# Preparation work handed out between the products of a pair, and loads spread over the steps of a block, in a two-layer kernel behind chunked attention

## The chip, the core and the metric

The kernel runs on one core of a Trainium2 chip. The metric is the device time of one execution in microseconds (us), as the median of several runs. The engines are named as in the profile: PE multiplies matrices, PEld is PE's weight load, DVE is the vector engine, ACT the scalar engine, POOL GpSimd. SP issues nearly all DMAs.

## The reference

Attention within chunks of 64 tokens over (8, 8, 576, 64), then two feed-forward layers on 4608 tokens, with a model width of 512 and an inner width of 2048. All arrays are float32 or float64.

```python
scores = scale * np.matmul(q_c, k_c.transpose(0, 1, 2, 4, 3))
attn = np.exp(scores - np.max(scores, axis=-1, keepdims=True))
attn = attn / (np.sum(attn, axis=-1, keepdims=True) + 1e-09)
x = np.matmul(attn, v_c)              # to 4608 x 512
h = x @ w1_in;  x = (h * np.cos(h)) @ w1_out
h = x @ w2_in;  y = (h / (1 + np.exp(-1.702 * h))) @ w2_out
```

## The kernel before, in words

**Tiles.** The 4608 tokens are nine blocks j of 512. The inner width is sixteen slices f of 128. A float32 factor is split into a high and a low part (`split`, lines 187 to 189: ACT copies the high part, DVE subtracts to get the low one), and each product is three matmuls, high x high, high x low, low x high, of 128 rows and 512 columns. `gemm1` (line 489) makes the 128 inner values of one slice, the activation follows on ACT and DVE, and `gemm2` (line 587) adds the slice's share of the output in four accumulators. Weights come as 64-bit numbers and are converted with a chain of seven closures (`split_w_parts`, lines 206 to 259: p0 on ACT at line 214, p1 to p4 on DVE, p5 on ACT, p6 on DVE).

**Order of the stages.** In layer 0 block 0 is laid out by a planner (`Plan`), blocks 1 and 2 are plain steps (gemm1 of a slice, activation, extra work, gemm2 of the slice two before). Blocks 3 and 4, 5 and 6, 7 and 8 are done jointly, in three rounds q = 0, 1, 2 (`by_1024`, line 880): eight pairs of slices (`pair_of_slices`, line 808), in which the two slices of two blocks need seven products in place of eight, and then sixteen steps with gemm2 alone for the second block of the two. Layer 1 has one plain block and four joint ones.

**A pair.** The products are made in the order 1, 0, 2, 3, 5, 4, 6, six matmuls each, in the PSUM tiles `pb`, `pu` and `pc` (line 820). Between them stands the fill: 24 matmuls of gemm2 of the pair before (`run(6)` after product 2, `run(10)` after 5, `run(8)` after 4). Products 0, 3, 4 and 6 all add to the same tile `pu`. So the sum c11 must be taken out of it before product 3 adds to it, the copy c12 before product 4, the sum c22 before product 6. The sums are DVE additions (`plus`, line 835, tile `part`), the copies ACT's (`copied`, line 831). Four activations follow (`act_second`, lines 787 to 793). The left factors of a pair (combinations of weights) are loaded from DRAM a pair ahead (`load_factors`, line 733); the right ones (combinations of x, `right_factor`, line 739) stay in SBUF for a round: b11, b21 and b22 are x itself, split, and t1 to t4 are differences (line 758), each formed and then split.

**Preparation.** The left factors of layer 1 are prepared during layer 0's pairs, in 24 slots (three rounds of eight pairs). Each of eight pairs of weight slices takes four stages in four slots, from slots 0, 2, 4, 8, 10, 12, 16, 18 (`PREP`, `prepare1`, line 715): load both slices, convert one, convert the other, form the factors and store them (`left_factors`, line 652, DVE at 664, store at 676). So slots 3, 5, 11, 13 and 19 hold the factors of one pair of slices and the conversion of another; slots 7, 15 and 21 hold factors alone. All of a slot's work stands behind its pair in the program. The factors of x for the first joint round come in step 13 (b22) and step 15 (the others) of block 2.

**What orders the queues.** PE's order is that of the program (`manual_schedule` for PE, by hand in the program). The compiler orders the other engines and SP. The scratch tiles `t`, `r`, `wt`, `su`, `sw`, `part`, `chain`, `yo` share eight buffers (pool `tmp`, tag t).

**The last round's steps.** In round q = 2, x of layer 1 is loaded and split, and weights of layer 1 are loaded: the input weights from the stored factors (`load_w1`, line 709, 14 of 16 slices in these steps), the first nine slices of the output weights raw (`load_w`, line 196), four of them converted. Layer 0's own output weights come three steps ahead (`load_wo`, line 700, into four tiles).

Of the kernel before, what the change touches and what calls it, by code (L numbers as in the profile page):

```python
# [9 lines left out]
F32 = mybir.dt.float32  # L10
# [9 lines left out]
P = 128  # L20
# [92 lines left out]
def tile_chunk_attention_two_moe(  # L113
# [29 lines left out]


    SJ1 = ((0, 3, 5), (7, 10, 12))
    SJ2 = ((0, 3, 4), (1, 5, 6), (7, 10, 11), (8, 12, 13))
    SJ3 = ((0, 3, 4), (1, 5, 6), (4, 7, 8), (5, 9, 10))
    SR = (8, 10)

# [37 lines left out]
    def split(hi, lo, src):  # L187
        nc.scalar.activation(out=hi, in_=src, func=AF.Copy)  # L188
        nc.vector.tensor_tensor(out=lo, in0=src, in1=hi.bitcast(F32), op=ALU.subtract)  # L189
# [433 lines left out]
    def at(key, fn, *args):  # L623
        extra.setdefault(key, []).append((fn, args))
# [27 lines left out]
    def left_factors(layer, i, t, parts):  # L652

        H2 = DM // 2
        u = tp.tile([P, DM], F32, tag="t", name="su")
        w = tp.tile([P, DM], F32, tag="t", name="sw")
        add, sub = ALU.add, ALU.subtract
        for o, x, y, op in (
            (u[:, :H2], t[1][:, :H2], t[1][:, H2:], add),
            (u[:, H2:], u[:, :H2], t[0][:, :H2], sub),  # L660
            (w[:, :H2], t[0][:, :H2], t[1][:, :H2], sub),
            (w[:, H2:], t[0][:, H2:], u[:, H2:], sub),
        ):
            nc.vector.tensor_tensor(out=o, in0=x, in1=y, op=op)
        todo = [(A11, parts[0]), (A21, parts[1])]
        for k, src in ((0, u), (1, w)):
            if layer == 0:
                hi, lo = (tp.tile([P, DM], F32R, tag="t", name="s_part") for _ in range(2))
            else:
                both = wp.tile([P, 2 * DM], F32R, tag=f"i{NF - 2 + k}", name="s_part")  # L670
                hi, lo = both[:, :DM], both[:, DM:]
            split(hi, lo, src)
            todo.append((A_S1 + 2 * k, (hi, lo)))
        for at_op, both in todo:
            for part in range(2):
                nc.sync.dma_start(
                    out=wc[layer][i][part, :, at_op:at_op + 2, :]
                    .rearrange("p o c -> p (o c)").bitcast(F32),
                    in_=both[part].bitcast(F32),
                )  # L680

    def left_factors0(i):
        parts = [W[0, "i", 2 * i + k] for k in range(2)]
        t = []
        for hi, lo in parts:
            x = tp.tile([P, DM], F32, tag="t", name="w32")
            nc.vector.tensor_tensor(out=x, in0=hi.bitcast(F32), in1=lo.bitcast(F32), op=ALU.add)
            t.append(x)
        left_factors(0, i, t, parts)

    def store_wo(f):
        hi, lo = W[0, "o", f]
# [22 lines left out]
    def prepare1(i, stage):  # L715

        fs = (2 * i, 2 * i + 1)
        for k, f in enumerate(fs):
            if stage == 0:
                load_w(w2_in, 1, "i", f, tag=f"o{k}")  # L720
            elif stage == 1 + k:
                for fn in split_w_parts(1, "i", f, False, tag=f"o{2 + k}"):
                    fn()
        if stage == 3:
            left_factors(1, i, [T.pop(f) for f in fs], [W[1, "i", f] for f in fs])

    LF = {}

# [32 lines left out]
    RIGHT = [(m, k) for m in (0, 1, 2, 3, 6, 5, 4) for k in range(2)]  # L761

    RIGHT_A = [(5, k) for k in range(2)]
    RIGHT_B = [(m, k) for k in range(2) for m in (1, 0, 2, 3, 6, 4)]

    PARK = {}

# [37 lines left out]
        if f < NF:  # L805
            split(*new_g((layer, j, f)), PARK.pop(f))

    def pair_of_slices(layer, ja, i, fill):

        jb = ja + 1  # L810
        f1, f2 = 2 * i, 2 * i + 1
        lf = LF.pop(i)

        def product(m, a, out, start, stop):
            for k in range(2):
                w = slice(k * P, (k + 1) * P)
                ah, al = lf[0][:, a, w], lf[1][:, a, w]
                bh, bl = RF[m][0][:, k], RF[m][1][:, k]
                for n, (x, y) in enumerate(((ah, bh), (ah, bl), (al, bh))):
                    nc.tensor.matmul(  # L820
                        out=out, lhsT=x, rhs=y,
                        start=(start and k == 0 and n == 0), stop=(stop and k == 1 and n == 2), skip_group_check=True,
                    )

        def run(count):
            for _ in range(min(count, len(fill))):
                fill.pop(0)()

        def copied(src):
            t = tp.tile([P, N], F32, tag="t", name="part")  # L830
            nc.scalar.activation(out=t, in_=src, func=AF.Copy)
            return t

        def plus(t, more):
            nc.vector.tensor_tensor(out=t, in0=more, in1=t, op=ALU.add)  # L835
            return t

        pk = park(layer, i)
        b = ps_a.tile([P, N], F32, tag="a", name="pb")
        product(1, A12, b, True, True)  # L840
        c11 = copied(b)
        u = ps_h.tile([P, N], F32, tag="h", name="pu")
        product(0, A11, u, True, False)
        c11 = plus(c11, u)
        c = ps_a.tile([P, N], F32, tag="a", name="pc")
        product(2, A_S1, c, True, False)
        c22 = copied(c)
        act_second(layer, jb, f1, c11, pk[0])
        run(6)
        product(3, A_S2, u, False, False)  # L850
        c12 = copied(u)
        product(5, A_S4, c, False, True)
        c12 = plus(c12, c)
        act_second(layer, ja, f1, c12)
        run(10)
        product(4, A_S3, u, False, False)
        c22 = plus(c22, u)
        act_second(layer, ja, f2, c22)
        run(8)
        product(6, A22, u, False, True)  # L860
        act_second(layer, jb, f2, u, pk[1])
        run(len(fill))

    for m, k in RIGHT:
# [9 lines left out]
    at((0, J0 - 1, 4), load_factors, 0, 0)  # L874
    for m, k in RIGHT_A:
        at((0, J0 - 1, 13), right_factor, 0, J0, m, k)
    for m, k in RIGHT_B:
        at((0, J0 - 1, 15), right_factor, 0, J0, m, k)

    def by_1024(layer, ja, rest, pair_extra, step_extra, last):  # L880

        jb = ja + 1
        for i in range(NP):
            if i + 1 < NP:
                load_factors(layer, i + 1)
            if layer == 0:
                for f in (2 * i, 2 * i + 1):
                    load_wo(f)
            pair_of_slices(layer, ja, i, [fn for m in rest for fn in gemm2_list(*m)])
            if i == 0:  # L890
                flush_y(*rest[-1][:2])
            for fn, args in pair_extra.get(i, []):
                fn(*args)
            rest = [(layer, ja, 2 * i), (layer, ja, 2 * i + 1)]
        if not last:
            load_factors(layer, 0)
        if layer == 0:
            load_wo(0)
            load_wo(1)
        split_park(layer, jb, 0)  # L900
        for m in rest:
            gemm2(*m)
        if layer == 0:
            load_wo(2)
        flush_y(layer, ja)
        for f in range(NF - LAG):
            if layer == 0 and f + 3 < NF:
                load_wo(f + 3)
            split_park(layer, jb, f + 1)
            for fn, args in step_extra.get(f, []):  # L910
                fn(*args)
            gemm2(layer, jb, f)
        split_park(layer, jb, NF - 1)
        return [(layer, jb, NF - 2), (layer, jb, NF - 1)]
# [187 lines left out]
    with tc.manual_schedule(engines={mybir.EngineType.PE}):  # L1102
# [21 lines left out]
        for q in range(3):  # L1124
            ja = J0 + 2 * q
            last = q == 2
            pair_extra, step_extra = {}, {}
            for i in range(NP):
                for stage in range(4):
                    if slots[PREP[i] + stage][0] == q:  # L1130
                        pair_extra.setdefault(slots[PREP[i] + stage][1], []).append(
                            (prepare1, (i, stage))
                        )
# [11 lines left out]
            else:  # L1145
                step_extra[0] = [(load_x1, (0,))]
                for k in range(KD):
                    step_extra.setdefault(3 + 3 * k, []).append((split_x1, (0, k)))
                for f in range(NF - LAG):
                    step_extra.setdefault(f, []).append((load_w1, (f,)))  # L1150
                for f in range(4):
                    step_extra.setdefault(f, []).append((load_w, (w2_out, 1, "o", f)))
                    step_extra.setdefault(2 * f + 4, []).append((split_w, (1, "o", f)))
                for f in range(4, 9):
                    step_extra.setdefault(2 * (f - 4) + 3, []).append((load_w, (w2_out, 1, "o", f)))
            rest = by_1024(0, ja, rest, pair_extra, step_extra, last)
        for f in range(NF - LAG, NF):
            at((1, 0, f - NF + LAG), load_w1, f)
        for f in range(4, NF):
            n = NB * NF + f - 4  # L1160
            at(steps[n], split_w, 1, "o", f)
# [59 lines left out]
```

## Time and profile before

| | us |
|---|---|
| median of 3 runs (1631.73 to 1631.95) | 1631.89 |
| the profiled execution, its own time | 1631.03 |
| its span | 1629.3 |
| PE busy | 1576.9 |
| DVE busy | 988.3 |
| ACT busy | 886.7 |

The span is the time between the first and the last instruction on the core. Matmuls overlap, and the profile gives one as 0.39 us though the next starts 0.23 us after it; PE's idle time and the distance of starts are therefore read, rather than the durations. In a timeline the first number is the start in us, the second how long the row lasts, x8 means eight instructions in the row, and brackets hold the idle time before it and what ended it.

### The profile page before, as it was taken

The numbers are of one execution on the slowest core, as the hardware profiler recorded it, in microseconds if no ns is written. First come the engines' busy times: TensorE is split into PE (matmuls) and PEld (weight loads), VectorE is DVE, ScalarE is ACT, GpSimd is POOL, SyncE is SP. The second block draws the span as 40 slices with busy tenths as digits, with TensorE's granted clock in tenths as the row PEclk, the third lists the DMA queues.
The fourth block names the chain that finished last, engine by engine and source line by source line (L and its number), as shares of the span: only waits on it lengthen the run. The fifth ranks groups of instructions, "written<-read, shape, count | busy, mean of one in ns | idle before, by whom it ended". The sixth has DMA issues, their size and how long they took to land.

```text
span 1629.3 us, 23504 instructions
## 1 busy us (share of the span) xinstructions
PE 1576.9 (97%) x9024; PEld 1295.0 (79%) x9024; DVE 988.3 (61%) x1621; ACT 886.7 (54%) x1545; POOL 42.2 (3%) x53
## 2 busy tenths in 40 slices
PE   5898999989999999999999999999999999999998
PEld 4677888878788877788787888888888888888887
DVE  7797657776887687867773844445444544454442
ACT  7787557667765677567773643334333433343332
POOL 1221000000000000000000100000000000000000
PEclk9899999999999999999999999999999999999999
DMA  9999234358887788957999525250535053504310
GB/s 357 338 301 315 91 105 142 118 184 285 299 302 299 249 290 268 362 188 274 327 319 344 136 72 207 113 196 2 205 112 199 2 202 113 200 3 175 114 74 26
DMA packets 99328, 322.14 MB, mean 198 GB/s; under 512 B 10768, under 2 KB 10768, under 8 KB 84880
## 3 DMA queue, kind: packets, MB, share of 16 engines
q1 hardware_dynamic: 92448, 308.32, 52.6%
q0 software_dynamic: 6768, 12.32, 4.2%
q8 instruction: 71, 1.16, 0.3%
q14 instruction: 41, 0.34, 0.1%
HBM read 247.46 MB, written 60.82 MB: 189 GB/s over the span
## 4 chain that ended last, share of the span: by engine, by line
PE 84%; DVE 6%; DMA 4%; ACT 3%; issue 2%; SPq 0%; POOL 0%; DVEq 0%; POOLq 0%; ACTq 0%
PE y L587 43%; PE pu L820 17%; PE pc L820 9%; PE h L489 9%; PE pb L820 4%; DMA raw_o<-w_out 1%; DMA i<-wt 1%; PE x L411 1%; PE s L304 1%; DVE r L788 1%; PE pt_ps L385 1%; DMA wo<-wo 1%; ACT r L792 1%; DVE r L793 1%; ACT r L791 1%
## 5 line engine op out<-in xcount | busy, mean ns | idle before, releaser
L587 PE MATMUL y<-o,gh 128*128 128x512 f32 x1152 | 299.3, 389 | 0.0
L587 PEld LDWEIGHTS y<-o,gh 128*128 128x128 f32 x1152 | 216.3, 188 | 44.9
L820 PE MATMUL pu<-x_t,w_xh 128*128 128x512 f32 x672 | 208.9, 392 | 10.4 <-DVE part L835 10.4
L587 PE MATMUL y<-gh,wo 128*128 128x512 f32 x768 | 202.9, 393 | 2.8 <-DMA wo<-wo 2.8
L587 PEld LDWEIGHTS y<-gh,wo 128*128 128x128 f32 x768 | 142.4, 188 | 33.6 <-issue 2.6
L587 PE MATMUL y<-o,gl 128*128 128x512 f32 x576 | 158.3, 389 | 0.0
L820 PEld LDWEIGHTS pu<-x_t,w_xh 128*128 128x128 f32 x672 | 125.9, 189 | 39.5 <-DVE part L835 9.1
L189 DVE TENSOR_TENSOR gl<-park,gh 128x512 fp32r<-128x512 f32 x112 | 76.8, 687 | 116.3 <-PE y L587 116.0
L489 PE MATMUL h<-xh,i 128*128 128x512 f32 x384 | 131.9, 406 | 15.6 <-DVE r L528 11.8
L188 ACT ACTIVATE gh<-park 128x512 fp32r<-128x512 f32 x112 | 70.3, 629 | 129.6 <-PE y L587 129.6
L820 PE MATMUL pu<-x_t,w_xl 128*128 128x512 f32 x336 | 131.3, 391 | 0.0
L587 PEld LDWEIGHTS y<-o,gl 128*128 128x128 f32 x576 | 108.1, 188 | 22.4
L797 ACT ACTIVATE r<-part 128x512 f32<-128x512 f32 x96 | 60.3, 629 | 93.9 <-DVE part L835 93.9
L835 DVE TENSOR_TENSOR part<-pu,part 128x512 f32<-128x512 f32 x112 | 77.2, 689 | 52.2 <-PE pu L820 49.6
L189 DVE TENSOR_TENSOR gl<-r,gh 128x512 fp32r<-128x512 f32 x112 | 77.4, 691 | 48.4 <-ACT gh L188 46.9
L587 PE MATMUL y<-gl,wo 128*128 128x512 f32 x384 | 105.9, 390 | 0.0
L188 ACT ACTIVATE gh<-r 128x512 fp32r<-128x512 f32 x112 | 70.8, 632 | 64.0 <-DVE r L798 50.9
L489 PEld LDWEIGHTS h<-xh,i 128*128 128x128 f32 x384 | 75.1, 196 | 34.6 <-DVE r L528 13.9
L587 PE MATMUL y<-gh,o 128*128 128x512 f32 x384 | 101.0, 401 | 0.0
L835 DVE TENSOR_TENSOR part<-pc,part 128x512 f32<-128x512 f32 x56 | 38.7, 691 | 89.2 <-PE pc L820 81.5
L587 PEld LDWEIGHTS y<-gl,wo 128*128 128x128 f32 x384 | 72.1, 188 | 15.6 <-DVE gl L189 0.7
L587 PEld LDWEIGHTS y<-gh,o 128*128 128x128 f32 x384 | 71.4, 191 | 15.1
(122 smaller groups left out, 2776.8 us busy)
## 6 DMA issues: line engine op xcount, KB each, us to landing
w_xh<-wc SPq DMA_DIRECT2D x56, 1024.0 KB, 5.9
w_xl<-wc SPq DMA_DIRECT2D x56, 1024.0 KB, 7.7
wo<-wo SPq DMA_DIRECT2D x96, 512.0 KB, 4.6
qk<-qk SPq DMA_DIRECT2D x36, 512.0 KB, 6.8
raw_i<-w_in SPq DMA_DIRECT2D x32, 512.0 KB, 7.3
raw_o<-w_out SPq DMA_DIRECT2D x32, 512.0 KB, 9.4
wc<-i SPq DMA_DIRECT2D x64, 256.0 KB, 5.5
wc<-s_part SPq DMA_DIRECT2D x64, 256.0 KB, 4.2
```

The lines of the kernel that those rows point to most:

```text
L188: nc.scalar.activation(out=hi, in_=src, func=AF.Copy)
L189: nc.vector.tensor_tensor(out=lo, in0=src, in1=hi.bitcast(F32), op=ALU.subtract)
L304: nc.tensor.matmul(out=s[e][o0:o0 + CH, w, h, :], lhsT=t[p0:p0 + CH, 0, h, o0:o0 + CH], rhs=t[p0:p0 + CH, 1, h, o0:o0 + CH],)
L385: nc.tensor.transpose(pt_ps[:, b, :], a[:, e, w, h0:h0 + 2, :].rearrange("p g k -> p (g k)"), ident)
L411: nc.tensor.matmul(out=xs[i][o0:o0 + CH, b, w, c * CH:(c + 1) * CH], lhsT=t[p0:p0 + CH, c, b, e, :], rhs=pt[p0:p0 + CH, e * (HP // 2) + b, ...
L489: nc.tensor.matmul(out=h, lhsT=a[:, w0], rhs=b[:, k, :], start=(k == 0 and i == 0), stop=(k == KD - 1 and i == 2),)
L587: nc.tensor.matmul(out=ys[d0], lhsT=a, rhs=b, start=(f == 0 and i == 0), stop=(f == NF - 1 and i == 2),)
L788: nc.vector.scalar_tensor_tensor(out=r, in0=h, scalar=INV_2PI, in1=n, op0=ALU.mult, op1=ALU.subtract)
L791: nc.scalar.activation(out=r, in_=r, func=AF.Sin, scale=math.pi)
L797: nc.scalar.activation(out=r, in_=h, func=AF.Sigmoid, scale=1.702)
L820: nc.tensor.matmul(out=out, lhsT=x, rhs=y, start=(start and k == 0 and n == 0), stop=(stop and k == 1 and n == 2), skip_group_check=True,)
L835: nc.vector.tensor_tensor(out=t, in0=more, in1=t, op=ALU.add)
```

## The change

The second layer's preparation is no longer called behind a pair. `prepare1` and `left_factors` return lists of closures, `by_1024` gathers those of a slot, and `pair_of_slices` calls a fifth of them (rounded up) at each of five places between its products. The factors of x for the first joint round are ordered by product instead of by half; six of the twelve come two each in steps 13, 14 and 15, the other six are handed out in the first pair. The stores of the combined factors come ahead of those of the plain ones. The last two units of attention in block 2 do their transposes and values one step earlier. In the last round the loads are put at other steps: ten slices of `load_w1` in steps 2 to 13 and six in the first steps of layer 1, the raw output weights in steps 1, 3, 5, 7 and 9 to 13.

```diff
-    SJ2 = ((0, 3, 4), (1, 5, 6), (7, 10, 11), (8, 12, 13))
+    SJ2 = ((0, 3, 4), (1, 5, 6), (7, 9, 10), (8, 11, 12))
...
     def left_factors(layer, i, t, parts):
...
+        return [
+            lambda: (sums(), one(0)),
+            lambda: one(1),
+            lambda: one(2),
+            lambda: one(3),
+            lambda: parts_of(0),
+            lambda: parts_of(1),
+            lambda: store(A11, parts[0]),
+            lambda: store(A21, parts[1]),
+        ]
...
     def prepare1(i, stage):
...
+        if stage == 0:
+            return [lambda k=k, f=f: load_w(w2_in, 1, "i", f, tag=f"o{k}") for k, f in enumerate(fs)]
+        if stage < 3:
+            return split_w_parts(1, "i", fs[stage - 1], False, tag=f"o{1 + stage}")
+        return left_factors(1, i, [T.pop(f) for f in fs], [W[1, "i", f] for f in fs])
...
-    RIGHT_B = [(m, k) for k in range(2) for m in (1, 0, 2, 3, 6, 4)]
+    RIGHT_B = [(m, k) for m in (1, 0, 2, 3, 4, 6) for k in range(2)]
...
-    def pair_of_slices(layer, ja, i, fill):
+    def pair_of_slices(layer, ja, i, fill, beside):
...
+        portion = -(-len(beside) // 5)
+
+        def aside():
+            for _ in range(min(portion, len(beside))):
+                beside.pop(0)()
...
         c11 = plus(c11, u)
+        aside()
         c = ps_a.tile([P, N], F32, tag="a", name="pc")
         product(2, A_S1, c, True, False)
         c22 = copied(c)
         act_second(layer, jb, f1, c11, pk[0])
+        aside()
         run(6)
...
         act_second(layer, ja, f1, c12)
+        aside()
         run(10)
         product(4, A_S3, u, False, False)
         c22 = plus(c22, u)
         act_second(layer, ja, f2, c22)
+        aside()
         run(8)
         product(6, A22, u, False, True)
         act_second(layer, jb, f2, u, pk[1])
+        aside()
         run(len(fill))
...
-    for m, k in RIGHT_B:
-        at((0, J0 - 1, 15), right_factor, 0, J0, m, k)
+    for n, (m, k) in enumerate(RIGHT_B[:6]):
+        at((0, J0 - 1, 13 + n // 2), right_factor, 0, J0, m, k)
...
-            pair_of_slices(layer, ja, i, [fn for m in rest for fn in gemm2_list(*m)])
+            beside = [fn for make, args in pair_extra.get(i, []) for fn in make(*args)]
+            pair_of_slices(layer, ja, i, [fn for m in rest for fn in gemm2_list(*m)], beside)
             if i == 0:
                 flush_y(*rest[-1][:2])
-            for fn, args in pair_extra.get(i, []):
-                fn(*args)
...
+                pair_extra[0] = [
+                    (lambda m, k: [lambda: right_factor(0, J0, m, k)], f) for f in RIGHT_B[6:]
+                ]
...
                 for k in range(KD):
-                    step_extra.setdefault(3 + 3 * k, []).append((split_x1, (0, k)))
-                for f in range(NF - LAG):
-                    step_extra.setdefault(f, []).append((load_w1, (f,)))
+                    step_extra.setdefault(4 + 3 * k, []).append((split_x1, (0, k)))
+                for f in range(10):
+                    step_extra.setdefault(2 + 5 * f // 4, []).append((load_w1, (f,)))
                 for f in range(4):
-                    step_extra.setdefault(f, []).append((load_w, (w2_out, 1, "o", f)))
-                    step_extra.setdefault(2 * f + 4, []).append((split_w, (1, "o", f)))
+                    step_extra.setdefault(2 * f + 1, []).append((load_w, (w2_out, 1, "o", f)))
+                    step_extra.setdefault(2 * f + 5, []).append((split_w, (1, "o", f)))
                 for f in range(4, 9):
-                    step_extra.setdefault(2 * (f - 4) + 3, []).append((load_w, (w2_out, 1, "o", f)))
+                    step_extra.setdefault(f + 5, []).append((load_w, (w2_out, 1, "o", f)))
...
-        for f in range(NF - LAG, NF):
-            at((1, 0, f - NF + LAG), load_w1, f)
+        for f in range(10, NF):
+            at((1, 0, f - 10), load_w1, f)
```

## Rows read from the trace of the kernel before

**Rows 1.** The page: busy us of each engine, share of the span, instructions.

```profile
PE 1576.9 (97%) x9024; PEld 1295.0 (79%) x9024; DVE 988.3 (61%) x1621; ACT 886.7 (54%) x1545; POOL 42.2 (3%) x53
```

**Rows 2.** Whom PE waited for, 336 to 835 us: total us, times, longest.

```profile
PE pu L820 <- DVE part L835: 10.4, 7, 4.3
...
PE s L304 <- DVE a L332: 1.0, 4, 0.3
```

**Rows 3.** Stretches, mostly pairs: length, busy us by engine, granted clock, DMA share, GB/s.

```profile
350.70:355.80 5.10, 5.07 (x16) 4.10 (x17) 2.38 (x4) 2.40 (x4) 0.00 (x0) 0.69 0.13 54
...
340.81:361.83 21.02, 16.70 (x67) 13.40 (x66) 15.72 (x26) 12.47 (x22) 0.00 (x0) 0.92 0.59 210
361.83:376.81 14.98, 14.98 (x67) 12.34 (x66) 9.57 (x15) 11.09 (x21) 0.00 (x0) 1.00 0.79 282
376.81:391.77 14.96, 14.96 (x67) 12.39 (x66) 11.11 (x18) 10.51 (x19) 0.00 (x0) 1.00 0.83 280
...
406.73:422.65 15.92, 15.25 (x67) 12.31 (x66) 13.09 (x24) 11.99 (x22) 0.00 (x0) 1.00 0.91 305
...
437.60:453.90 16.30, 15.14 (x67) 12.21 (x66) 13.04 (x23) 12.33 (x23) 0.00 (x0) 1.00 0.90 286
```

**Rows 4.** PE's timeline: the first pair's fill and product 3, a later product 3.

```profile
344.89 1.52 PE L587 MATMUL y<-gh,o 128*128 128x512 f32 x6
350.73 1.19 PE L820 MATMUL pu<-x_t,w_xh 128*128 128x512 f32 x2 [4.32 <-DVE part L835]
...
444.38 0.73 PE L820 MATMUL pu<-x_t,w_xh 128*128 128x512 f32 x2 [1.16 <-DVE part L835]
```

**Rows 5.** Timelines of ACT (the first row) and DVE around the first pair.

```profile
328.65 1.19 ACT L450 ACTIVATE xs<-x 128x256 f32<-128x256 f32 x4
...
330.99 2.49 DVE L189 TENSOR_TENSOR x_b<-xs,x_b 128x512 fp32r<-128x512 f32 x4
...
339.07 0.68 DVE L758 TENSOR_TENSOR chain<-xs 128x512 f32<-128x512 f32 x1
...
349.90 0.68 DVE L835 TENSOR_TENSOR part<-pu,part 128x512 f32<-128x512 f32 x1
```

**Rows 6.** Timelines of DVE and PE (the second row) in two later pairs.

```profile
389.29 0.69 DVE L835 TENSOR_TENSOR part<-pu,part 128x512 f32<-128x512 f32 x1
...
390.41 0.61 PE L820 MATMUL pu<-x_t,w_xh 128*128 128x512 f32 x2
...
411.94 0.42 DVE L217 TENSOR_SCALAR wt<-wt 128x512 f32<-128x512 f32 x1
412.27 0.68 DVE L835 TENSOR_TENSOR part<-pu,part 128x512 f32<-128x512 f32 x1
```

**Rows 7.** ACT's timeline at the end of a pair.

```profile
392.61 0.58 ACT L787 ACTIVATE r<-pu 128x512 int32<-128x512 f32 x1
393.08 0.66 ACT L214 ACTIVATE wt<-raw_i 128x512 f32<-128x512 f32 x1
```

**Rows 8.** Whom SP's queue waited for, 320 to 880 us.

```profile
SPq L196 <- DVE wt L234: 44.8, 10, 5.4
```

**Rows 9.** Timelines of DVE and PE: a normalisation and step 9 of block 2.

```profile
296.40 1.21 DVE L362 TENSOR_TENSOR a<-a,ss 128x1024 f32<-128x1024 f32 x1
...
301.02 1.98 PE L587 MATMUL y<-gh,o 128*128 128x512 f32 x8
```

**Rows 10.** The last round's steps: SP, PE, and DMA issues 848 to 852 (KB, us to landing).

```profile
849.52 1.24 SPq L196 DMA_DIRECT2D raw_o<-w_out  x1
...
854.55 2.08 PE L587 MATMUL y<-gh,wo 128*128 128x512 f32 x8
...
859.75 2.09 PE L587 MATMUL y<-gh,wo 128*128 128x512 f32 x8 [2.22 <-DMA wo<-wo]
...
863.30 2.08 PE L587 MATMUL y<-gh,wo 128*128 128x512 f32 x8 [0.54 <-DMA wo<-wo]
...
wo<-wo SPq DMA_DIRECT2D x2, 512.0 KB, 10.9
```

More of the change, by code (lines that the diff above doesn't have):

```diff
@@ L654, in left_factors, with sums, one, store @@
         H2 = DM // 2
[L655 to L663, printed above, removed]
-            nc.vector.tensor_tensor(out=o, in0=x, in1=y, op=op)
[L665 to L674, printed above, removed]
+        c = {}
+        def sums():
+            c["u"] = tp.tile([P, DM], F32, tag="t", name="su")
+            c["w"] = tp.tile([P, DM], F32, tag="t", name="sw")
+        def one(k):
+            u, w = c["u"], c["w"]
+            add, sub = ALU.add, ALU.subtract
+            o, x, y, op = (
+                (u[:, :H2], t[1][:, :H2], t[1][:, H2:], add),
+                (u[:, H2:], u[:, :H2], t[0][:, :H2], sub),
+                (w[:, :H2], t[0][:, :H2], t[1][:, :H2], sub),
+                (w[:, H2:], t[0][:, H2:], u[:, H2:], sub),
+            )[k]
+            nc.vector.tensor_tensor(out=o, in0=x, in1=y, op=op)
+        def store(at_op, both):
             for part in range(2):
@@ L680, in left_factors, with parts_of @@
                 )
+        def parts_of(k):
+            if layer == 0:
+                hi, lo = (tp.tile([P, DM], F32R, tag="t", name="s_part") for _ in range(2))
+            else:
+                both = wp.tile([P, 2 * DM], F32R, tag=f"i{NF - 2 + k}", name="s_part")
+                hi, lo = both[:, :DM], both[:, DM:]
+            split(hi, lo, c["uw"[k]])
+            store(A_S1 + 2 * k, (hi, lo))
+        return [
[8 more added lines that the diff above has]
+        ]
     def left_factors0(i):
@@ L688, in left_factors0 @@
             t.append(x)
-        left_factors(0, i, t, parts)
+        for fn in left_factors(0, i, t, parts):
+            fn()
     def store_wo(f):
@@ L717, in prepare1 @@
         fs = (2 * i, 2 * i + 1)
[L718 to L725, printed above, removed]
+        if stage == 0:
[3 more added lines that the diff above has]
+        return left_factors(1, i, [T.pop(f) for f in fs], [W[1, "i", f] for f in fs])
     LF = {}
@@ L1127, in tile_chunk_attention_two_moe @@
             pair_extra, step_extra = {}, {}
+            if q == 0:
+                pair_extra[0] = [
+                    (lambda m, k: [lambda: right_factor(0, J0, m, k)], f) for f in RIGHT_B[6:]
+                ]
             for i in range(NP):
```

## The prediction, made before the changed kernel was run

> **What bounds the kernel now.** I read first the busy line of the page [rows 1]: PE works 97% of the span, so only PE's gaps and PE's own work can set the time, and the change leaves PE's work as it is. Then the list of whom PE waited for [rows 2]: between 336 and 835 us, the joint blocks of the first layer, it waited 10.4 us in seven waits for one thing, the addition `part` of line 835, the longest 4.3 us; the six others make 6.1 us. Then the length of each pair of slices [rows 3]. A pair is 42 product matmuls and 24 of the fill; undisturbed it takes 14.96 us, so 0.227 us per matmul. The first takes 21.02, which is 6.06 too many, and the two after slots 3 and 5 take 15.92 and 16.30, so 0.96 and 1.34 too many. The reader should see that the excess is larger than the recorded wait. In the first pair the fill of six ends at 344.89 + 6 x 0.227 = 346.25 and product 3 starts at 350.73 [rows 4]; the clock granted in the stretch after it is 0.69, a mixture of the 1.2 and 2.4 GHz levels, while the pairs with the short waits keep 1.00 [rows 3]. In these each wait costs some 0.2 us of restart (1.34 against 1.16 [rows 3, 4]). The six are so worth 6.1 + 6 x 0.2 = 7.3 us. Last, DVE's order of work shows why. In the first pair the addition stands at 349.90, behind a row of chain differences and their splits that begins at 339.07 [rows 5]. In the pair at 406.73 it stands at 412.27, directly behind the first `wt` operation of the conversion, 411.94 [rows 6], and PE needed it by 412.1.
>
> One more thing decides. ACT's `wt` of a stage comes right after the last `r` of the pair, 393.08 after 392.61 [rows 7]: both are tiles of the eight of tag t, which are given out in the order of the program. So a stage written behind a pair can't begin before that pair's end, however idle DVE was, and the next pair's first copy waits for the stage's tiles. PE's order is as written; the other queues are laid out by the compiler with the program's order as priority (a raw load at 849.52, in step 4 of its block, is the one written for step 7 [rows 10]).
>
> **The change part by part.**
> *The preparation handed out in portions.* Nothing is added or removed: a stage of conversion is 7 closures, the factors 8, and slots 3, 5, 11, 13 and 19 have both (portions of 3; elsewhere 2). The `wt` tile is now asked for right after the pair's first copy, so the chain begins about 13 us earlier and in lighter pairs runs through the pair's first half. What is left over for the next pair is at most 3 closures, two DVE operations of 0.6 us (four take 2.49 [rows 5]), where up to 15 stood. The addition c11 then has its inputs 3.1 us into the pair and product 3 comes at 5.44: 2.3 us for at most two operations and itself. The six waits go: -7.3. What is late next is the other addition, c22, before product 6: in a light pair it runs from 389.29 to 389.98 and product 6 starts at 390.41 [rows 6], so 0.43 us is free. One 0.6 us operation caught in front of it costs 0.17, two cost 0.77. For the six slots behind which PE waited I take 0.2 each (one caught), +1.2. For the other 13 slots with conversions or factors I take 0.1, as their chain is mostly over by then: +1.3, with ends 0 and 13 x 0.77 = 10.0.
>
> *Its DMAs.* Each preparation issues 2 raw loads and 8 stores on SP, now written inside the pair. A raw load that waits for the raw tile's last reader stands in front of SP's other issues; that is so today, 44.8 us in ten waits, the longest 5.4 [rows 8], and no product waited for a factor load. A factor load is issued some 15 us before its pair. Cost 0; without that cover, up to 5.4 us where a load of factors stands behind.
>
> *First joint block.* The last two units' transposes and values come one step earlier. For the first of them step 9's slot is at 301.02 and its normalisation, begun at 296.40, is over at 297.6 [rows 9]: 3.4 us to spare, cost 0. The staging of x that ends at 329.8 then ends about 6 us earlier, and the four b11 and b21 splits at 330.99 [rows 5] move into idle time. Of the 12 factors of x six remain ahead of the pair; t2, t3, t4 (12 DVE operations, 7.2 us) go into its first three portions, each ahead of the product that reads it. From 339.07 DVE then has until product 3: the step's own three operations, t1 (4), c11, t2 (4), 12 x 0.6 = 7.2, so 346.3 against product 3 at 346.25: 0.05 late. From there until product 6: t3 (4), the activations of two slices (4), c12, t4 (4) and c22, 14 x 0.6 = 8.4, so 354.7 against 340.81 + 13.6 = 354.4: 0.3 late. ACT's part in these chains adds something; I take 0.8 us, ends 0 and 3.0 (half the loss). Gain 6.06 - 0.8 = 5.3, the clock's share with it, since no long gap is left.
>
> *Softmax at the start of the block after.* Four waits of PE for line 332, 1.0 us [rows 2], stand behind leftovers of the last slot's factors. These are now done within the pair. I take half, -0.5 (ends 0 and -1.0).
>
> *Loads spread.* In the last block's 2.72 us steps two matmul groups of the fill wait for `wo`: from 854.55 to 859.75 and on to 863.30, 8.75 us for two steps of 2.72, 3.3 too many [rows 10]. Loads of `wo` issued at 848 to 852 took 10.9 us to land [rows 10] and only 8.2 us (three steps) are there. What stands before them are raw loads that were issued as soon as their tile was free, up to three steps ahead of where they are written. Writing them later by six steps leaves the tile free at the same time; only their rank against other waiting loads changes. I take 0, with ends -3.3 (the wait goes) and +2.3, as the last block gets there 2.3 us earlier (its two waits go) with the same bytes to move.
>
> **Sum** against the profiled execution, 1631.03 (span 1629.3 and 1.7 around it): -7.3 + 1.2 + 1.3 - 5.3 - 0.5 + 0 = -10.6, so 1620.4. The median of the runs is 0.9 above the profiled one: 1621.3.
>
> **Rivals.**
> *The loads do spread.* `wo` no longer waits: -3.3 more, 1618.0. For it: rank is program order, and raw loads now rank behind more. Against: the one at 849.52 was far ahead of its place [rows 10]. Chance 0.17.
> *The scratch tiles are the limit.* Six gaps of nearly one size could come from the eight t tiles rather than from DVE's order: now two difference tiles, or the factors' two, are held inside the pair beside `wt` and the pair's own five or so. Then only the first pair gains: 1631.0 - 5.3 + 0.9 = 1626.6. For it: `wt` begins where the last `r` was given out [rows 7]. Against: DVE was busy without a gap in front of the late additions [rows 5, 6]. The Trainium skill ("Perfetto Trace Analysis", Optimization Strategy) says that the same gap repeating on the engine that should be full can mean too few buffers for the next tile; by it this rival, not my forecast, would be read from these gaps, and no row here counts tiles in use. Chance 0.13.
> *Slower: the portions get in front of c22.* Portion operations rank above the rest of their pair. If in all 19 slots that convert or form factors three of them stand in front of c22, each pair waits 3 x 0.6 - 0.43 = 1.37 us: +26.0 against -12.6 for the old waits (7.3 and 5.3), 1645.3. It decides from 12.6 / 19 = 0.66 us per pair; slower by 0.2% needs 0.84. For it: 0.43 us of slack is little, and DVE was busy 13.09 of 15.92 us in a full pair [rows 3]. Against: c22 needs the 0.7 us only, and while its product runs the portion has mostly nothing ready. Chance 0.06.
> *The compiler's order undoes it*: it moves portions so that about as much is lost as won, 1630. Chance 0.04.
>
> **How the numbers follow.** The forecast has 0.60. The predicted time is 1621.3. The range reaches down to where the loads' end (-3.3) and the lower ends of the terms for c22 (-2.5) come together: 1615.5, and up past the scratch rival, with one operation caught in each of the 13 other slots beside it (13 x 0.17 = 2.2): 1628.8. About 0.2% (3.3 us) is what a measurement of this kernel can tell from no change: 1628.6 to 1635.2 is same. Faster: the forecast, the loads, and most of the scratch rival, 0.85; same 0.09; slower 0.06.
>
> **What would show it.** Right: the first pair at 340.8 lasts about 15.8 us with the granted clock at 1.00 throughout; the waits of `pu` for line 835 fall from 10.4 to under 3 us, and what is left stands before product 6; `wt` operations lie within the pair; DVE is idle for less of 322 to 331. Wrong: additions c11 still behind `wt` or `su`; new waits of 0.5 us or more in most pairs; a wait of PE for `qk`, `pt` or `a` in steps 9 to 12; gaps before `wo` of more than 3 us.

## The result, and the profile after

The changed kernel takes **1615.20 us** (median of 4 runs, 1614.17 to 1616.25) against 1631.92 for the kernel before in the same runs: a ratio of 0.9898, 95% interval 0.9880 to 0.9915. That is 16.7 us less, where the prediction had 10.6, and 0.3 us below the range. The profiled execution took 1616.11, its span 1614.3; against the span of before that is 15.0 us.

The page's busy line answers to [rows 1]: the work is the same, the same number of instructions on each engine. Of the 15.0 us, 12.8 are PE's idle time (52.4 to 39.6 us of the span), and 2.2 its busy time, of which the first pair, no longer at a lower clock, has 1.7 (16.70 to 14.96).

```profile
PE 1574.7 (98%) x9024; PEld 1294.2 (80%) x9024; DVE 989.0 (61%) x1621; ACT 885.1 (55%) x1545; POOL 42.2 (3%) x53
```

Whom PE waited for between 336 and 835 us: the list of [rows 2] is down to one row, the attention's `pt`. The seven waits for `part`, 10.4 us, and the four for `a` are gone.

```profile
PE s L304 <- ACT pt L392: 1.1, 4, 0.4
```

The stretches of [rows 3] (length, PE's busy time, granted clock, DMA share, GB/s). The first pair has the length of an undisturbed one, the clock at 2.4 GHz throughout; so has the pair behind slot 3 (401.73). The last row is a pair with something left.

```profile
341.77:356.73 14.96, 14.96 (x68) 1.00 0.83 293
...
401.73:416.69 14.96, 14.96 (x68) 1.00 0.91 321
416.69:431.96 15.27, 15.26 (x68) 1.00 0.91 309
```

PE's timeline of the first pair, the place of [rows 4]: product 3 starts when the six matmuls of fill are through, with no bracket.

```profile
345.85 1.52 PE L587 MATMUL y<-gh,o 128*128 128x512 f32 x6
347.21 0.62 PE L837 MATMUL pu<-x_t,w_xh 128*128 128x512 f32 x2
```

DVE's timeline there, answering to [rows 5]: the start of the chain of differences, the sum c11, the sum c22. From the chain's start to c11's end are 6.8 us, where before 11.5 lay between them; c11 is ready at 346.34, 0.87 us ahead of product 3, and c22 at 354.45, 0.9 ahead of product 6 (355.37).

```profile
339.52 0.69 DVE L774 TENSOR_TENSOR chain<-xs 128x512 f32<-128x512 f32 x1
...
345.65 0.69 DVE L858 TENSOR_TENSOR part<-pu,part 128x512 f32<-128x512 f32 x1
...
353.76 0.69 DVE L858 TENSOR_TENSOR part<-pu,part 128x512 f32<-128x512 f32 x1
```

ACT's timeline, answering to [rows 7]: a stage's `wt` now begins 4.2 us into the pair that starts at 356.73, not behind its last `r`.

```profile
360.94 0.67 ACT L214 ACTIVATE wt<-raw_i 128x512 f32<-128x512 f32 x1
```

The pair of 15.27 us, DVE and then PE: c22 stands behind a conversion step and an activation step, ends at 430.40, and product 6 starts at 430.46 where 430.29 would be undisturbed. With the restart that makes 0.31 us; the same happens in slot 13 (595.40 to 610.66), and in no other pair.

```profile
428.51 0.69 DVE L228 SCALAR_TENSOR_TENSOR wt<-raw_i,wt 128x512 uint32<-128x512 uint32 x1
429.12 0.68 DVE L809 SCALAR_TENSOR_TENSOR r<-r,part 128x512 f32<-128x512 f32 x1
429.72 0.68 DVE L858 TENSOR_TENSOR part<-pu,part 128x512 f32<-128x512 f32 x1
...
430.46 0.73 PE L837 MATMUL pu<-x_t,w_xh 128*128 128x512 f32 x2
```

The last round's steps, answering to [rows 10]: the wait of 2.22 us for `wo` is 0.71 now.

```profile
844.54 2.06 PE L587 MATMUL y<-gh,wo 128*128 128x512 f32 x8 [0.71 <-DMA wo<-wo]
847.77 2.09 PE L587 MATMUL y<-gh,wo 128*128 128x512 f32 x8 [0.27 <-DMA wo<-wo]
```

From the starts of PE's pairs in both profiles, the 15.0 us are:

| stretch | before | after | difference |
|---|---|---|---|
| start of the first pair | 340.81 | 341.77 | +0.96 |
| first pair | 21.02 | 14.96 | -6.06 |
| the other pairs, rounds 0, 1, 2 | 307.39 | 300.22 | -7.17 |
| steps after rounds 0 and 1 | 148.42 | 147.27 | -1.15 |
| last pair's start to layer 1's first joint pair | 149.14 | 147.50 | -1.64 |
| from there to the end | 662.52 | 662.58 | +0.06 |

The first row is scatter: in the four profiles whose program ahead of the first pair is that of the kernel before, the pair starts between 340.2 and 341.6 us, over all sixteen between 339.8 and 342.1, at 340.5 in the changed kernel without its loads.

### The profile page after: what moved, and what is told of

It reads as the page before. It is cut to its first block, busy times and chain, and to the rows that moved or that the text cites. A ratio compares the mean times of both kernels' runs of the same rounds, so it can differ in the third digit from the quotient of the medians.

```text
span 1614.3 us, 23505 instructions
## 1 busy us (share of the span) xinstructions
PE 1574.7 (98%) x9024; PEld 1294.2 (80%) x9024; DVE 989.0 (61%) x1621; ACT 885.1 (55%) x1545; POOL 42.2 (3%) x53
## 3 DMA queue, kind: packets, MB, share of 16 engines
q8 instruction: 71, 1.16, 0.3%
## 4 chain that ended last, share of the span: by engine, by line
PE 92%; DMA 2%; issue 2%; ACT 2%; DVE 1%; SPq 0%; POOL 0%; POOLq 0%; DVEq 0%; ACTq 0%
PE y L587 47%; PE pu L837 19%; PE pc L837 9%; PE h L489 9%; PE pb L837 5%; PE x L411 1%; PE pt_ps L385 1%; PE s L304 1%; DMA i<-wt 1%; DMA raw_o<-w_out 1%; DMA wo<-wo 1%; ACT a L352 0%; DVE wt L234 0%; ACT a L340 0%; DVE wt L228 0%
## 5 line engine op out<-in xcount | busy, mean ns | idle before, releaser
L489 PE MATMUL h<-xh,i 128*128 128x512 f32 x384 | 132.3, 407 | 15.1 <-DVE r L528 10.1
L587 PEld LDWEIGHTS y<-gh,o 128*128 128x128 f32 x384 | 71.8, 192 | 15.3
```

The costliest lines, as they stand in the source:

```text
L489: nc.tensor.matmul(out=h, lhsT=a[:, w0], rhs=b[:, k, :], start=(k == 0 and i == 0), stop=(k == KD - 1 and i == 2),)
L587: nc.tensor.matmul(out=ys[d0], lhsT=a, rhs=b, start=(f == 0 and i == 0), stop=(f == NF - 1 and i == 2),)
```

## The experiments

The theory: each part acts by itself; the pairs gain by their stage starting inside the pair, the first pair by six factors being taken from ahead of product 3, the loads by nothing. Each number below is the median of runs beside runs of the kernel before on the same chip (1631.0 to 1632.5 in the four series), with the ratio to those.

**Only the portions** (the units, the factors of x and the loads of the kernel before).

```diff
-    SJ2 = ((0, 3, 4), (1, 5, 6), (7, 9, 10), (8, 11, 12))
+    SJ2 = ((0, 3, 4), (1, 5, 6), (7, 10, 11), (8, 12, 13))
...
-    RIGHT_B = [(m, k) for m in (1, 0, 2, 3, 4, 6) for k in range(2)]
+    RIGHT_B = [(m, k) for k in range(2) for m in (1, 0, 2, 3, 6, 4)]
...
-                    (lambda m, k: [lambda: right_factor(0, J0, m, k)], f) for f in RIGHT_B[6:]
...
```

> The second layer's preparation is handed out within the pairs; attention's steps, the factors of x and the loads stay as before. Theory A (each part cures its own wait): the six waits before product 3 in the later pairs go (-7.2 us in the lengths of the pairs, two of them now 15.3 for a late c22), the wait for softmax goes (-1.1), the first pair stays at 21.0, and the wait for wo stays at 3.3 us, so about 1623.5. Theory B (wo waited for the backlog that the preparation's stores and loads leave, and handing them out is what relieved it): besides, the wait for wo falls to about 1.6, 1622.

1621.76, ratio 0.9940 (0.9927 to 0.9954). The six short waits and the softmax waits are gone; four pairs are left with a late c22 (15.25 to 15.34 us). The wait for `wo` fell as well, to 0.70 and 0.28 us, and the stretch from the last pair's start to layer 1's first joint pair to 147.06: the number of theory B, whose reason the next experiment doesn't bear out. The first pair keeps its wait, and it costs more than before: the same 4.32 us, but the 5.1 us from product 3 on lie wholly at the lower clock level, 0.50, where [rows 3] had 0.69, and the pair takes 22.24. The timeline of PE, then the stretch (busy times in the order PE, PEld, DVE, ACT, POOL, then clock, DMA share, GB/s):

```profile
350.37 1.19 PE L837 MATMUL pu<-x_t,w_xh 128*128 128x512 f32 x2 [4.32 <-DVE part L858]
```

```profile
350.35:355.45 5.10, 5.08 (x12) 4.04 (x13) 1.85 (x3) 2.39 (x4) 0.00 (x0) 0.50 0.16 66
```

**Only the first block** (units, six factors in three steps, six in the first pair; the preparation behind its pair again, the loads as before).

```diff
-            beside = [fn for make, args in pair_extra.get(i, []) for fn in make(*args)]
+            beside = [fn for make, args in parts if make is not prepare1 for fn in make(*args)]
...
+            for make, args in parts:
+                if make is prepare1:
+                    for fn in make(*args):
+                        fn()
...
```

> Attention's two units a step earlier and the factors of x in three steps and in the first pair; the preparation stands behind the pair and the loads are as before. Theory A: the first pair falls from 21.0 to 14.96 us, -6.1, the six waits, softmax's and wo's stay: about 1625.9. Rival (the first pair was only in part DVE's and something else, the clock or the first pair's loads, keeps 1 to 3 us): 1627 to 1629.

1625.46, ratio 0.9965 (0.9951 to 0.9978). The first pair takes 14.96, the six waits stand as before, 6.6 us in all, and so do those of the softmax. The wait for `wo` is short here too (0.81 and 0.69, the stretch 147.53), though the preparation stands behind its pair as before. The two parts alone bring 9.2 and 5.5 of the 16.7 us. They can't simply be added: each holds the shorter stretch in front of layer 1 (2.1 and 1.6 us), which the changed kernel has once, and the first has a first pair 1.2 us longer than that of [rows 3].

**Only the loads.**

```diff
-                for f in range(NF - LAG):
-                    step_extra.setdefault(f, []).append((load_w1, (f,)))
+                for f in range(10):
+                    step_extra.setdefault(2 + 5 * f // 4, []).append((load_w1, (f,)))
...
```

> The loads of the last round are spread as in the change, nothing else. Theory A: the waits for wo fall from 3.3 to about 1.6 us, 1630.3. Theory B (spreading changes only the rank, and a load still goes out as soon as its tile is free): waits for wo as before within 0.5 us, 1631.5 to 1632.5.

1631.05, ratio 1.0000 (0.9991 to 1.0009), and the wait for `wo` is 2.20 us, as theory B had it.

**All but the loads**, the other side of the same question.

> The changed kernel with the loads of the last round where the kernel before has them. Theory (spreading the loads is worth nothing, and the shorter wait for wo comes by itself): 1614 to 1616.5, its time within 1 us of the changed kernel's 1615.2, and the last round's steps with layer 1's plain block (last pair's start to the first pair of layer 1) 147 to 148 us. Rival (the spread loads bring the 1.6 us that this stretch lost): 1616.5 to 1617.5, the stretch 149 us with a wait for wo of some 2 us.

1614.49, ratio 0.9893 (0.9878 to 0.9909): the loads bring nothing, though the wait for `wo` is short here too (0.56 and 0.54, the stretch 147.19).

**The preparation in tiles of its own, nothing moved**: `wt`, `su` and `sw` in the attention's tiles, in the kernel before.

```diff
-            c["t"] = tp.tile([P, DM], F32, tag="t", name="wt")
+            if layer == 1 and which == "i":
+                if f % 2 == 0:
+                    both = ap.tile([P, 2 * G, CH], F32, tag="a", name="wt")
+                    OWN[f // 2] = both.rearrange("p g k -> p (g k)")
+                c["t"] = OWN[f // 2][:, f % 2 * DM:(f % 2 + 1) * DM]
...
```

> The kernel before, with one edit: the preparation's scratch (wt, su, sw) lies in the tiles that attention's softmax uses between the rounds, and no longer in the eight that the pairs share. Nothing is moved in the program. If it is the order in which the shared tiles are given out that held a stage back until the end of its pair, the compiler now starts it within the pair, the six waits go and it comes to about 1624 (softmax's -1.1 with it: 1623.5). If DVE's rank by program order alone puts a stage in front of c11, the six waits stay: 1631.9.

1629.57, ratio 0.9993 (0.9984 to 1.0002). The waits before product 3 in the six pairs behind slots 3, 5, 11, 13, 19 and 21 disappear, so the order in which scratch tiles are given out did hold the stages back to the pair's end. But the time stays: beside the first pair's there are 13 waits for `part` now, before products 3 and 6 and mostly in other pairs, and the pairs behind the first take 2.7 us more than before (310.05 for 307.39). The stretch in front of layer 1 is short here too, 147.48. The waits between 336 and 835 us, then two of them in one pair of 17.37 us:

```profile
PE pu L829 <- DVE part L844: 11.7, 14, 4.3
```

```profile
385.73 0.73 PE L829 MATMUL pu<-x_t,w_xh 128*128 128x512 f32 x2 [1.11 <-DVE part L844]
394.90 0.73 PE L829 MATMUL pu<-x_t,w_xh 128*128 128x512 f32 x2 [0.72 <-DVE part L844]
```

So an early start alone is worth nothing in the pairs. Whether what counts is where in the pair it comes, the next two ask directly.

**The whole list at the first place**, right behind the sum c11, and **the whole list at the third**, in front of c22 (`== 3`). The first joint pair keeps its portions of two.

```diff
-        portion = -(-len(beside) // 5)
+        place = [0]
...
+            place[0] += 1
+            portion = len(beside) if place[0] == 1 else 0
+            if layer == 0 and ja == J0 and i == 0:
+                portion = 2
```

> The changed kernel, but a slot's whole list of closures is called at the first place, right after the sum c11; only the first joint pair keeps portions of two. Theory A (what counts is that the stage may start inside the pair, and that its chain of dependent steps lets the pair's own sums in; 10 us lie between this place and c22): 1615 to 1617, no wait over 0.4 us before products 3 or 6. Rival B (portions are needed: up to 15 operations in one go stand before c12 or c22): 1619 to 1625, with waits of 0.5 to 1.2 us before product 6 in the five slots that have both factors and a conversion.

> As the kernel before this one, but the whole list is called at the third place, behind c12's activation and in front of c22. Theory A as there: the chain begins later, runs past the pair's end and is what the next pair's sum c11 then finds in front of it: some 1616 to 1619, waits of 0.3 to 0.7 us before product 3 or 6 in a few slots. Rival B (the whole list gets in front of c22, the mechanism of the slower rival): waits of 0.7 us or more before product 6 in at least ten of 19 slots, 1623 or more.

First place: 1613.71, ratio 0.9888 (0.9874 to 0.9901), against 1614.49 for all but the loads in the same series, no difference clear of noise. No pair is longer than 15.1 us, the 0.31 us of slots 5 and 13 are gone too. In the pair of slot 3, a heavy one (with the factors of one pair of slices and the conversion of another), which starts at 384.86, c22 on DVE and product 6 on PE are 0.92 us apart:

```profile
396.85 0.69 DVE L862 TENSOR_TENSOR part<-pu,part 128x512 f32<-128x512 f32 x1 [0.32 <-PE pu L837]
...
398.46 0.62 PE L837 MATMUL pu<-x_t,w_xh 128*128 128x512 f32 x2
```

Third place: **1637.68**, ratio 1.0039 (1.0027 to 1.0052): slower than before, with the first pair at 14.96. Of the 20 pairs behind it whose length shows from start to start, 17 are over 15.3 us, up to 18.84; together they are 21 us too long, where the list of waits has 14.0. Whom PE waited for, and the same heavy slot, which starts at 386.46 here: after c22's product is through, at 398.4, two steps of the pair's own (one ahead of these rows, and `gl`) and three of the list (`s_part`, `wt`, `wt`) run ahead of c22, and product 6 waits 2.36 us.

```profile
PE pu L837 <- DVE part L862: 14.0, 9, 2.4
```

```profile
399.43 0.69 DVE L189 TENSOR_TENSOR s_part<-sw,s_part 128x512 fp32r<-128x512 f32 x1
400.03 0.69 DVE L228 SCALAR_TENSOR_TENSOR wt<-raw_i,wt 128x512 uint32<-128x512 uint32 x1
400.63 0.69 DVE L189 TENSOR_TENSOR gl<-r,gh 128x512 fp32r<-128x512 f32 x1
401.24 0.69 DVE L234 SCALAR_TENSOR_TENSOR wt<-raw_i,wt 128x512 uint32<-128x512 uint32 x1
401.84 0.69 DVE L862 TENSOR_TENSOR part<-pu,part 128x512 f32<-128x512 f32 x1
...
402.58 0.73 PE L837 MATMUL pu<-x_t,w_xh 128*128 128x512 f32 x2 [2.36 <-DVE part L862]
```

Both kernels run the same operations. In the first, c11 ended at 389.07 in that pair and c22 starts at 396.85, so 7.8 us lie between the place and c22. In the second, c12 ended at 395.58, and product 4, after which c22 can start, ends 12 us into the pair, at 398.4: 3 us lie between. The other places weren't tried with whole lists.

**The kernel before, profiled again.** The prediction had put `wo` at no change, and it fell even without the spread loads.

> The kernel before, unchanged, profiled once more. Theory (the wait for wo varies from one execution to the next by itself): the waits for wo in the last round's steps differ from the 2.2 and 0.5 us of the first profile by 0.5 us or more, and the stretch from the last pair's start to layer 1's first pair from 149.1 by as much. Rival (it belongs to the program): 2.0 to 2.4 us again and 149.0 to 149.3. The first joint pair: 21.0 to 22.3 us.

One run, 1631.93. The wait is the same 2.22 us, and the stretch 149.13, so it belongs to the program. PE's timeline, first pair and `wo`:

```profile
351.54 1.19 PE L820 MATMUL pu<-x_t,w_xh 128*128 128x512 f32 x2 [4.32 <-DVE part L835]
...
860.67 2.08 PE L587 MATMUL y<-gh,wo 128*128 128x512 f32 x8 [2.22 <-DMA wo<-wo]
```

**The low parts of the first four output slices on DVE** in place of POOL's accumulating DMAs, with the whole list at the first place and in the changed kernel.

```diff
-        for fn in split_w_parts(layer, which, f, layer == 1):
+        for fn in split_w_parts(layer, which, f, layer == 1 and not (which == "o" and f < 4)):
```

> Whole lists at the first place, and the low parts of the second layer's first four output slices formed on DVE in place of POOL's four accumulating DMAs. Theory (the wait for wo is the DMA engines' load at that point, of which the accumulating DMAs take about half for some 8 us): no wait for wo over 0.3 us, 1.2 us less than with whole lists at the first place alone, 1612.0 to 1612.8 against 1613.7. Rival (DVE, busy 3.8 of 4 us there, delays the last steps' splits and the wait only changes its name): within 0.5 us of 1613.7, with waits for gh or part in place of wo. Second rival (wo waits for something else than bytes): waits for wo of 1.0 to 1.5 us as before.

> The changed kernel with those low parts on DVE. Theory: 1.1 us less than the changed kernel, 1614.1 against 1615.2, and no wait for wo over 0.3 us. Rival: 1615 with the same waits or with others in their place.

1611.91, ratio 0.9883 (0.9867 to 0.9900), and 1613.25, ratio 0.9890 (0.9875 to 0.9905). No wait for `wo` is left in either; the stretch is 145.52 in both, 2.0 us less than in the changed kernel. The same eight microseconds, 26 to 34 us behind the start of the last pair, first in the changed kernel and then with the low parts on DVE (columns as above): POOL's 3.45 us of issuing are gone, and at much the same DMA share 382 and 347 GB/s are moved in place of 344 and 270. DVE, at 3.99 of 4 us, has just the room.

```profile
830.22:834.22 4.00, 4.00 (x20) 3.30 (x19) 4.00 (x10) 3.06 (x6) 1.73 (x2) 1.00 0.98 344
834.22:838.22 4.00, 4.00 (x19) 3.30 (x18) 2.04 (x4) 3.18 (x6) 1.72 (x2) 1.00 1.04 270
```

```profile
828.73:832.73 4.00, 4.00 (x19) 3.30 (x19) 3.99 (x9) 1.51 (x3) 0.00 (x0) 1.00 1.01 382
832.73:836.73 4.00, 4.00 (x20) 3.30 (x18) 3.86 (x7) 1.81 (x4) 0.00 (x0) 1.00 0.96 347
```

In the medians this gain is not clear of noise: the intervals overlap with those of the whole list at the first place and of the changed kernel (0.9888 and 0.9898). By its median the first of the two is the fastest version of the study, 19.1 us below its before where the changed kernel is 16.7 below.

**The first block's two halves**: the units alone (in the kernel before, `SJ2` of the changed one), and the factors of x alone (the first-block kernel with `SJ2` of before).

> The kernel before with the last two units of attention one step earlier, and nothing else. Theory (the late row of twelve factors is what holds the first pair; x being staged 6 us sooner lets only the four b11 and b21 splits move, since all twelve are still written into step 15 and their tiles are given out in that order): the first pair 18 to 21.5 us, 0 to 3 us of the 6.1 gained, median 1628.5 to 1632. Rival (the units alone do it): first pair under 15.8, 1625 to 1626.

> The kernel before with the factors of x for the first round ordered by product, six in three steps and six inside the first pair, the units of attention where they were. Theory (six factors inside the pair take 7.2 us from ahead of product 3, which was 4.3 us late): the first pair 14.96 to 15.8, 1625 to 1626.5, so the units' part of the change is worth 0.5 us at most. Rival (x comes too late without the earlier units: the staging ended at 329.8, b21, b11 and t1 still stand in a row behind it): a wait of 1 us or more before product 3 or 0, first pair 16.2 to 19.

Units: 1630.72, ratio 0.9998 (0.9989 to 1.0007), first pair 20.65. Factors: 1625.20, ratio 0.9962 (0.9949 to 0.9975), first pair 14.96, and a wait of 0.18 us in the pair after. PE's timelines, units alone and factors alone:

```profile
349.52 1.10 PE L820 MATMUL pu<-x_t,w_xh 128*128 128x512 f32 x2 [3.81 <-DVE part L835]
```

```profile
360.81 0.74 PE L837 MATMUL pu<-x_t,w_xh 128*128 128x512 f32 x2 [0.18 <-DVE part L858]
```

The gain of the first block is the factors'; x is staged early enough without the units' move, but for the 0.5 us by which that next pair is too long (15.47). With the factors alone the wait for `wo` is 1.14 us and the stretch 147.49; with the units alone 2.20 and 148.52.

**The order of the stores**, which the kernels with a short wait for `wo` had in common but for the one with own tiles: the new order alone in the kernel before, the old one alone in the changed kernel.

```diff
-        todo = [(A11, parts[0]), (A21, parts[1])]
+        todo = []
...
-        for at_op, both in todo:
+        for at_op, both in todo + [(A11, parts[0]), (A21, parts[1])]:
```

> The kernel before with the stores of the combined factors ahead of those of the plain ones, and nothing else. Theory (the order of the stores, which the loads of layer 1's weights read back, is what takes the wait for wo from 2.2 us to 0.6 to 1.1): first wait for wo under 1.2 us, the stretch from the last pair's start to layer 1's first pair 147.0 to 147.7 in place of 149.1, everything else as before, 1629.2 to 1630. Rival (something else in the new closures): a first wait of 2.2 us, the stretch 149, 1631.

> The changed kernel with the stores of the plain factors first again, handed out in the seventh and eighth place of each list before the splits. Theory: a first wait for wo of 2 us or more and the stretch 149 us, 1616.5 to 1617. Rival (the order of the stores plays no part): first wait 0.5 to 1.1, stretch 147 to 147.6, 1614 to 1616.

1631.77, ratio 1.0001 (0.9991 to 1.0010), wait 2.22; and 1614.13, ratio 0.9893 (0.9876 to 0.9909), waits 0.44 and 0.75. The order of the stores plays no part in the wait or the time.

## Why the prediction was right in its direction and short by six microseconds

**The six waits before product 3** (-7.3). Right in place, a little low in size. The waits are gone. From start to start the six pairs were 7.9 us too long, not 7.3: the prediction took 16.30 us for the pair at 437.60 from a window of [rows 3] that ends 0.14 us before the next pair starts. PE's timeline has the two starts 16.42 us apart, so a wait of 1.16 cost 1.46, with 0.3 us of restart where 0.2 was counted.

```profile
437.62 0.62 PE L820 MATMUL pb<-x_b,w_xh 128*128 128x512 f32 x2
...
454.04 0.62 PE L820 MATMUL pb<-x_b,w_xh 128*128 128x512 f32 x2
```

The portions alone take 6.7 us out of the pairs behind the first; the rest of their 9.2 is softmax (1.3), the stretch in front of layer 1 (2.1) and an earlier start (0.4), less the 1.2 that their first pair is longer. The reason held as well: a stage could not begin before its pair's end because of the order of the scratch tiles, and tiles of its own free it.

**c22 before product 6** (+1.2 and +1.3). This is the step that failed most: the prediction set one operation in front of c22 wherever a chain was about, six times 0.2 us and thirteen times 0.1. The pairs other than the first lost 7.17 us where -7.3 + 2.5 = -4.8 was forecast; of the 7.9 only 0.8 came back, 0.31 of it in each of two pairs. In all others c22 starts 11.98 to 12.89 us into the pair, and 12.91 is soon enough, as product 6 comes at 13.60 and c22 takes 0.69. A conversion alone or factors alone are mostly through by then or leave c22 in time. In the five slots with both, three steps of the conversion run ahead of c22. They are the tenth to twelfth closures, written at the fourth place and so behind c22 in the program; on DVE they come while c22's product is still being made. Three times c22 still starts at 12.55, in time, as in slot 3 (pair at 386.77), and twice at 13.03.

```profile
398.11 0.69 DVE L228 SCALAR_TENSOR_TENSOR wt<-raw_i,wt 128x512 uint32<-128x512 uint32 x1
...
399.32 0.69 DVE L858 TENSOR_TENSOR part<-pu,part 128x512 f32<-128x512 f32 x1
```

The margin is thin, and that only two pairs pay is in part luck: slot 15 has 0.02 us to spare, and with the portions alone four pairs pay. The mechanism is real: with the whole list at the third place it costs 21 us, 1.2 per lengthened pair, near the 1.37 per pair of the slower rival, and the kernel is slower than before. What was mis-sized is how often five portions bring it about. The prediction should have gone through the places of the list one by one, as it did for the first pair.

**The first pair** (-6.06 + 0.8). The chain took 6.8 us for the 7.2 counted, and it began 2.25 us ahead of the pair where before it was 1.74, so that c11 was 0.87 us early where 0.05 late was forecast. That is no matter of the later start: with whole lists at the first place the pair starts at 339.88, and c11 comes as far into it. Nothing was lost, -6.06. DVE was busy for 5.17 of the 9 us from 322 to 331 where it had been for 3.38, as the prediction had it. That the units' earlier stages cost nothing was right; they bring no measurable time either, which the prediction did not say.

**The softmax** (-0.5). All of it went, -1.15: the half held back was not needed. The new order of the factors of x holds in rounds 1 and 2 as well; it is not what did this, as the portions alone, with the old order, lose as much (147.15 us for these steps).

**The loads** (0). Right for the edit itself: alone it changes nothing, and undoing it changes nothing. Wrong for the stretch, which lost 1.64 us. Neither the loads, nor the units, nor the order of the stores does it alone, nor is it chance: the unchanged kernel shows 2.22 us twice, and each of the three has 2.2. The portions alone, the factors of x alone and tiles of its own for the preparation each bring it (147.06, 147.49, 147.48), and no single edit is common to these three. What the DMA engines carry there makes the wait, since it goes with the accumulating DMAs. In the first-block kernel SP issues the same loads at the same distances from the last pair's start, and the `wo` load issued 26 us behind it lands in 4.0 us, where the kernel before needs 6.6. What the three edits do to the DMA engines' work there is **open**.

By the sum: 2.4 (0.6 for the six waits, 1.7 for c22) + 0.8 + 0.65 + 1.64, less the 0.96 of a late start, are 4.5 of the 6.1 us between forecast and median; the rest is that the profiled execution of before lies 0.9 below its median and that of after 0.9 above. The lower end of the range took in the loads' end and c22's reserve, not those of the first pair and the softmax, 0.8 and 0.5; with them it would have been 1614.2. The case in which nothing came late was not reckoned through.

**The rivals.** *Scratch tiles the limit*: fell, since the eight tiles hold the stages inside the pairs. The rule of the Trainium skill ("Perfetto Trace Analysis", Optimization Strategy), that gaps repeating at one size can mean too few buffers, was half borne out: more tiles removed these gaps, of 0.7 to 1.2 us, but the time stayed at 0.9993 of before, as others came. *Loads spread*: fell. *Portions in front of c22*: in two pairs of 19 here, but it is what the place decides.

## What to carry to other kernels

Work for a later stage that is handed in between has to be placed by the deadline it might miss: behind a sum that the tensor engine waits for, and as far ahead of the next such sum as there is room. The same list costs 24 us more when it is called two places later (1637.7 for 1613.7), and cutting it into portions was not what made it cheap. Freeing a stage with more buffers, without saying when it may run, only moved the waits; and a stretch with the DMA engines full is the place to take a transfer out, not to write the same ones later.

## What was not expected of the hardware

The same wait of 4.32 us cost the first pair 6.1 us in two profiles of the kernel before and 7.3 in two other kernels: the granted clock in the 5.1 us after it was 0.69 and 0.67 in the former, a mixture of the two levels, and 0.50, the lower level throughout, in the latter (portions alone, loads alone). With the new order of the stores alone it cost 6.2, at 0.67.

The kernel before takes 1629.3 to 1633.0 us from run to run. In four profiles whose program ahead of the first pair is the same, that pair's start varies by 1.4 us (340.2 to 341.6), so part of the scatter arises ahead of it.
